# The second product of a spectral mixer and feed-forward kernel: its 21 matmuls per round in threes instead of two passes

## The chip, the cores and the metric

The kernel runs on one core of a Trainium2 chip. A time is the device time of one execution in microseconds (us). Three timed executions took 2598.35, 2600.91 and 2601.14 us; their median, 2600.91 us, is the time before. A fourth execution was recorded by the hardware profiler, and every line of a profile below comes from that one.

## The reference

Two stages follow each other. The first takes x (8 sequences of 3008 tokens, 256 channels), goes to the frequency domain along the tokens, applies one complex 256x256 matrix with a bias and a soft threshold, and goes back. The second is a feed-forward layer on the 24064 tokens:

```python
X = np.fft.rfft(x, axis=1)
Yr = Xr @ w_r - Xi @ w_i + b_r
Yi = Xr @ w_i + Xi @ w_r + b_i
Yr = np.sign(Yr) * np.maximum(np.abs(Yr) - lam, 0.0)   # Yi likewise
y = np.fft.irfft(Y, n=x.shape[1], axis=1)
h = np.maximum(y @ w_in, 0.0)        # 256 -> 2048
out = h * h @ w_out                  # 2048 -> 256
```

## The kernel before

**Operands in two parts.** A float32 operand is split into a high part, rounded to the fast matmul format (fp32r), and a low part, the rest. A product is then three matmuls into the same place of PSUM: high x high, high x low, low x high. The helper `mm3` (L179 to L184) issues them in that order: L182 the high stationary with the high moving operand, L183 the high stationary with the low moving one, L184 the low stationary with the high moving one. The first product of the feed-forward layer, the forward transform (`psa`), the mix (`psm1`, `psm2`) and the way back (`psc`) all go through it, so all their matmuls have the lines L182 to L184 in a profile.

**Rounds.** The tokens are cut into 47 chunks of 512. The hidden 2048 features are cut into 8 pairs of 128-feature blocks. One round is one pair of blocks for one chunk: 47 x 8 = 376 rounds, and one Python loop writes the instructions of every engine in the order in which they are to stand. There is no scheduler behind it; each engine works off its own list in order, and semaphores hold an instruction back until its operands are there and its buffer is free. A round r holds:

- the first product `mm1` into `ph`, two PSUM banks: 12 matmuls of 128x512;
- on ScalarE, `squares`: two relus out of `ph` (L877) and a square (L878) into the tile `g`;
- the second product `mm2` of round r - 3 into `po`, 21 matmuls of 128x256;
- on VectorE, `sums` (L883 to L885), which make the seven operands of a Strassen-like scheme out of `g`;
- on ScalarE `high` (L932), which casts `g` of round r - 1 into `gh`, and on VectorE `low` (L937), which takes the rest into `gl`.

The second product needs 7 sub-products instead of 8 for a 2x2 block product. `PLACES` lists them with their place in the four PSUM banks `po0` to `po3`: two in each of the first three, one in the last. `wo_[0]` and `wo_[1]` are the high and low parts of the combined weights, tiles of 128x7x128 per pair of blocks, in the profile `wo`. `gh` and `gl` have two buffers each, so the cast of round r - 1 goes into the buffer that the product of round r - 3 reads:

```python
def opnd(name, dt, bufs):
    return tl(name, (P, NPR, HALF), dt, bufs=bufs)
```

At a chunk's last round `put_together` copies and adds the seven places into the output tiles (one copy on ScalarE, L903, then seven sums on VectorE, L904 to L910) and sends them out. Bank by bank the last reader is L905 for the first, L906 for the second, L909 for the third and L910 for the fourth; the next chunk's first `mm2` writes the same banks.

**Work around the products.** The transform stage of the next sequences is spread over the rounds by a table and a small planner: places named `p1` (after the first product) and `p2` (after the second) take the matmuls of `psa`, `psb`, `psc`, `psd` and of the mix, and places `e`, `e2`, `f`, `f2`, `a`, `v` take the ScalarE and VectorE steps that belong to them. These matmuls share two PSUM buffers. A pair of frequency rows goes through `psb` in round r0, the mix (18 matmuls of 128x256) in round r0 + 2 and `psc` some rounds later. The mix's first bank is freed by the VectorE sum L233, which stands behind `gl` (L937) in its round. ScalarE's steps of such a round stand behind `gh` (L932): the copy of `psc` (L758), the cast to `xh` (L712), the turns into `z` (L740, L741), the cast to `zh` (L745) and the cast to `fh` (L668).

Of the kernel before, what the change touches and what calls it, by code (L numbers as in the profile page):

```python
# [130 lines left out]
PLACES = ((0, 0, 0), (2, 0, 1), (6, 1, 0), (5, 1, 1), (4, 2, 0), (3, 2, 1), (1, 3, 0))  # L131
NPR = 7
NU = NF // 2
# [3 lines left out]
HALF = CH // 2  # L137
# [12 lines left out]
def fft_mix_moe(ctx: ExitStack, tc: tile.TileContext, xp, xu, w_r, w_i, b_r, b_i,  # L150
                w_in, w_out, t_u, t_a, t_b, t_b0, t_m, t_d, sgn, outT):
    nc = tc.nc
# [19 lines left out]
    wo_ = [], []  # L172
# [6 lines left out]
    def mm3(out, lt, rt, start, stop, **kw):  # L179

        (l0, l1), (r0, r1) = lt, rt
        nc.tensor.matmul(out, l0, r0, start=start, stop=False, **kw)  # L182
        nc.tensor.matmul(out, l0, r1, start=False, stop=False, **kw)  # L183
        nc.tensor.matmul(out, l1, r0, start=False, stop=stop, **kw)  # L184
# [702 lines left out]
    def mm2(j, po, gh, gl):  # L887

        for s, bank, half in PLACES:
            out = po[bank][:, half * HALF:half * HALF + HALF]  # L890
            for k in range(2):
                nc.tensor.matmul(out, wo_[k][j][:, s], gh[:, s], start=j == 0 and half == 0 and k == 0,  # L892
                                 stop=False, skip_group_check=True)
        for s, bank, half in PLACES:
            out = po[bank][:, half * HALF:half * HALF + HALF]
            nc.tensor.matmul(out, wo_[0][j][:, s], gl[:, s], start=False, stop=j == NU - 1,  # L896
                             skip_group_check=True)

    def put_together(c, po):
        p = {s: po[bank][:, half * HALF:half * HALF + HALF] for s, bank, half in PLACES}  # L900
# [15 lines left out]
    with tc.manual_schedule():  # L916
        for r in range(last + LAG):
            c, j = divmod(r, NU)
# [6 lines left out]
            k = r - LAG  # L925
# [15 lines left out]
            if k >= 0:  # L941
                if jj == 0:
                    pos[cc] = [ps_o.tile([P, 512], F32, tag=f"o{i}", name=f"po{i}") for i in range(4)]
                mm2(jj, pos[cc], *split_.pop(k))
# [54 lines left out]
```

## Time and profile before

| | |
|---|---|
| median of three executions | 2600.91 us (2598.35 to 2601.14) |
| the profiled execution | 2604.28 us, span 2602.5 us |
| granted TensorE clock over the span | 0.992 |
| TensorE matmuls, busy | 2540.2 us, 98% |
| VectorE, ScalarE, GpSimd busy | 81%, 77%, 2% |
| DMA queue q1 | 161.91 MB, 20.1% of 16 engines |

The span runs from the first to the last instruction. In a group of instructions the columns are: line, engine, operation, the tile written and the tiles read, shapes, count, then busy time and mean ns of one, then the idle time of the engine just before them and who ended most of it. A row of the timeline has the start in us, the duration in us, the engine, the line, the operation with its tiles, and in brackets the idle time of the engine before it with its releaser; "x14" merges instructions that follow each other. Matmuls overlap, so what one costs is read from the distance of two starts, not from its duration. PEld is the loading of the stationary operand, which runs beside the matmul before it. A row of the waits has the total in us, the number of times and the longest.

### The profile page before, as it was taken

Reading aid. Unit: us, or ns where it says so; the run is one execution under the profiler, and the core shown is the slowest. Engines: PE = TensorE matmul, PEld = TensorE weight load, DVE = VectorE, ACT = ScalarE, POOL = GpSimd, SP = SyncE. Lnnn points to the kernel's source line nnn. Section 1 sums busy time; section 2 is a strip of 40 time slices with the busy share of each in tenths; the row PEclk is TensorE's granted clock in tenths of the full one; section 3 lists DMA queues with packets and bytes.
Section 4 is the critical chain, followed back from the end, with each engine's and each line's share of the span. In section 5 each row is a group of like instructions: output and inputs, shape, how many; then the busy total and the mean of one; then the engine's idle time right before and its main releaser. Section 6 shows DMA issues by size and latency. Waiting matters only on the chain.

```text
span 2602.5 us, 41936 instructions
## 1 busy us (share of the span) xinstructions
PE 2540.2 (98%) x16496; PEld 2284.6 (88%) x16496; DVE 2107.2 (81%) x3155; ACT 1993.8 (77%) x2764; POOL 47.9 (2%) x57
## 2 busy tenths in 40 slices
PE   6979999999999999999999999999999999999999
PEld 3569999999899998999889998899989898999998
DVE  4868888888888888888888888788887888777776
ACT  3668887788778787778877887778777777777776
POOL 1410000000000000000000000000000000000000
PEclk8999999999999999999999999999999999999999
DMA  8621122222221112111122112121121111100000
GB/s 252 186 84 57 49 73 65 78 60 64 76 67 53 55 56 76 57 54 52 57 78 63 55 54 68 56 67 60 44 72 53 41 37 57 37 27 28 20 24 17
DMA packets 113094, 164.59 MB, mean 63 GB/s; under 512 B 9584, under 2 KB 63074, under 8 KB 112706
## 3 DMA queue, kind: packets, MB, share of 16 engines
q1 hardware_dynamic: 112898, 161.91, 20.1%
q8 instruction: 131, 2.15, 0.3%
q14 instruction: 65, 0.53, 0.1%
HBM read 86.90 MB, written 74.97 MB: 62 GB/s over the span
## 4 chain that ended last, share of the span: by engine, by line
PE 82%; DVE 6%; ACT 5%; issue 1%; DMA 1%; DVEq 0%; SPq 0%; ACTq 0%
PE po L892 21%; PE ph L182 12%; PE ph L184 12%; PE ph L183 12%; PE po L896 11%; PE psd L268 3%; PE psb L219 3%; PE psm L182 2%; PE psm L183 2%; PE psm L184 2%; DVE gl L937 2%; ACT g L877 1%; DMA din<-s 1%; ACT g L878 1%; DVE g L883 1%
## 5 line engine op out<-in xcount | busy, mean ns | idle before, releaser
L937 DVE TENSOR_TENSOR gl<-g,gh 128x1792 fp32r<-128x1792 f32 x376 | 760.3, 2022 | 33.8 <-ACT gh L932 24.8
L877 ACT ACTIVATE g<-ph 128x512 f32<-128x512 f32 x752 | 409.2, 596 | 456.0 <-PE ph L184 454.5
L892 PE MATMUL po<-gh,wo 128*128 128x256 f32 x5264 | 700.9, 283 | 1.4 <-DVE o L909 0.8
L892 PEld LDWEIGHTS po<-gh,wo 128*128 128x128 f32 x5264 | 656.6, 188 | 15.1 <-DVE o L909 4.3
L932 ACT CAST gh<-g 128x1792 fp32r<-128x1792 f32 x376 | 638.4, 1698 | 19.9 <-PE po L892 16.6
L182 PE MATMUL ph<-xt,wi 128*128 128x512 f32 x1504 | 592.3, 394 | 11.2 <-DVE dx L276 8.7
L184 PE MATMUL ph<-xt,wi 128*128 128x512 f32 x1504 | 588.2, 391 | 0.0
L183 PE MATMUL ph<-xt,wi 128*128 128x512 f32 x1504 | 587.5, 391 | 0.0
L883 DVE TENSOR_TENSOR g<-g 128x512 f32<-128x512 f32 x376 | 260.0, 691 | 328.2 <-ACT g L878 325.9
L878 ACT ACTIVATE g<-g 128x1024 f32<-128x1024 f32 x376 | 399.5, 1062 | 11.9
L896 PE MATMUL po<-gl,wo 128*128 128x256 f32 x2632 | 371.3, 280 | 0.0
L184 PEld LDWEIGHTS ph<-xt,wi 128*128 128x128 f32 x1504 | 282.7, 188 | 64.4
L182 PEld LDWEIGHTS ph<-xt,wi 128*128 128x128 f32 x1504 | 282.9, 188 | 62.2 <-ACT xt L280 8.8
L896 PEld LDWEIGHTS po<-gl,wo 128*128 128x128 f32 x2632 | 336.8, 188 | 0.0
L183 PEld LDWEIGHTS ph<-xt,wi 128*128 128x128 f32 x1504 | 282.9, 188 | 50.5
L885 DVE TENSOR_TENSOR g<-g 128x256 f32<-128x256 f32 x376 | 160.0, 425 | 12.9
L884 DVE TENSOR_TENSOR g<-g 128x256 f32<-128x256 f32 x376 | 159.9, 425 | 12.8
L182 PE MATMUL psm<-wm,xh 128*128 128x256 f32 (+1 forms) x552 | 161.4, 292 | 3.7 <-DVE dx L276 3.2
L183 PE MATMUL psm<-wm,xh 128*128 128x256 f32 (+1 forms) x552 | 159.2, 288 | 0.0
L184 PE MATMUL psm<-wm,xl 128*128 128x256 f32 (+1 forms) x552 | 159.0, 288 | 0.0
L219 PEld LDWEIGHTS psb<-tB,bin 128*128 128x128 f32 x768 | 100.6, 194 | 36.0 <-issue 17.8
L268 PEld LDWEIGHTS psd<-tD,din 120*128 120x128 f32 (+1 forms) x832 | 107.4, 191 | 19.1 <-DMA din<-s 8.9
(102 smaller groups left out, 2569.7 us busy)
## 6 DMA issues: line engine op xcount, KB each, us to landing
bin<-s SPq DMA_DIRECT2D x96, 256.0 KB
s<-evc SPq DMA_DIRECT2D x96, 256.0 KB
outT_dram<-o SPq DMA_DIRECT2D x94, 256.0 KB
din<-s SPq DMA_DIRECT2D x96, 240.0 KB
xin<-in_xp_dram SPq DMA_DIRECT2D x72, 240.0 KB
s<-eva SPq DMA_DIRECT2D x72, 240.0 KB
s<-eva SPq DMA_DIRECT2D x22, 192.0 KB
w<-in_moe_w_in_dram SPq DMA_DIRECT2D x8, 512.0 KB
```

What stands on the lines that cost most here:

```text
L182: nc.tensor.matmul(out, l0, r0, start=start, stop=False, **kw)
L183: nc.tensor.matmul(out, l0, r1, start=False, stop=False, **kw)
L184: nc.tensor.matmul(out, l1, r0, start=False, stop=stop, **kw)
L219: nc.tensor.matmul(ps[:, k, :, q, :], tv[:, q, k], tB[:, 0:r + 2:r + 1], start=True, stop=True)
L268: nc.tensor.matmul(ps[:, k, part], t[:n, s:s + P], tD[:n, tab + part, :n], start=True, stop=True)
L877: nc.scalar.activation(g[:, 2 * a:2 * a + 2], ph[:, a].rearrange("p (t m) -> p t m", t=2), AF.Relu)
L878: nc.scalar.activation(g[:, 0:4], g[:, 0:4], AF.Square)
L883: nc.vector.tensor_sub(g[:, 4:6], g[:, 1:4:2], g[:, 0:2])
L892: nc.tensor.matmul(out, wo_[k][j][:, s], gh[:, s], start=j == 0 and half == 0 and k == 0, stop=False, skip_group_check=True)
L896: nc.tensor.matmul(out, wo_[0][j][:, s], gl[:, s], start=False, stop=j == NU - 1, skip_group_check=True)
L932: nc.scalar.copy(split_[r - 1][0], hid[r - 1])
L937: nc.vector.tensor_sub(gl, hid.pop(r - 1), gh.bitcast(F32))
```

## The change

`mm2` issued its 21 matmuls in two passes: first, place by place, the high and the low weights with the high operand `gh` (14 matmuls, L892), then the high weights with the low operand `gl` (7 matmuls, L896). Now it issues three per place through `mm3`. The matmuls are the same; their order is not. The place on which the first matmul of a chunk clears its bank and the one that ends it are set by the same conditions as before.

```diff
     def mm2(j, po, gh, gl):
 
         for s, bank, half in PLACES:
-            out = po[bank][:, half * HALF:half * HALF + HALF]
-            for k in range(2):
-                nc.tensor.matmul(out, wo_[k][j][:, s], gh[:, s], start=j == 0 and half == 0 and k == 0,
-                                 stop=False, skip_group_check=True)
-        for s, bank, half in PLACES:
-            out = po[bank][:, half * HALF:half * HALF + HALF]
-            nc.tensor.matmul(out, wo_[0][j][:, s], gl[:, s], start=False, stop=j == NU - 1,
-                             skip_group_check=True)
+            mm3(po[bank][:, half * HALF:half * HALF + HALF], (wo_[0][j][:, s], wo_[1][j][:, s]),
+                (gh[:, s], gl[:, s]), j == 0 and half == 0, j == NU - 1, skip_group_check=True)
```

The lines behind it move up by six: L932 and L937 of before are L926 and L931 afterwards.

TensorE at the end of a second product, here the last one of the kernel; `wo07` is the high and `wo17` the low part of the weights of pair 7. Before:

```order
L892 MATMUL po3_26309<-gh_26515,wo07_1097 128x256
L892 MATMUL po3_26309<-gh_26515,wo17_1098 128x256
L896 MATMUL po0_26306<-gl_26516,wo07_1097 128x256 x2
L896 MATMUL po1_26307<-gl_26516,wo07_1097 128x256 x2
L896 MATMUL po2_26308<-gl_26516,wo07_1097 128x256 x2
L896 MATMUL po3_26309<-gl_26516,wo07_1097 128x256
```

With the change:

```order
L184 MATMUL po2_26308<-gh_26515,wo17_1098 128x256
L182 MATMUL po2_26308<-gh_26515,wo07_1097 128x256
L183 MATMUL po2_26308<-gl_26516,wo07_1097 128x256
L184 MATMUL po2_26308<-gh_26515,wo17_1098 128x256
L182 MATMUL po3_26309<-gh_26515,wo07_1097 128x256
L183 MATMUL po3_26309<-gl_26516,wo07_1097 128x256
L184 MATMUL po3_26309<-gh_26515,wo17_1098 128x256
```

The last reader of `gh` was the 14th matmul of the 21 and is now the 21st; the last of `gl` was the 21st and is now the 20th. The first reader of `gl` was the 15th and is now the 2nd.

TensorE in the first product of the last chunk, where the banks come free one after the other. Before, from the 7th matmul on:

```order
L892 MATMUL po1_26307<-gh_26201,wo00_719 128x256
L892 MATMUL po1_26307<-gh_26201,wo10_720 128x256
L892 MATMUL po2_26308<-gh_26201,wo00_719 128x256
L892 MATMUL po2_26308<-gh_26201,wo10_720 128x256
L892 MATMUL po2_26308<-gh_26201,wo00_719 128x256
```

With the change, from the 10th on:

```order
L182 MATMUL po1_26307<-gh_26201,wo00_719 128x256
L183 MATMUL po1_26307<-gl_26202,wo00_719 128x256
L184 MATMUL po1_26307<-gh_26201,wo10_720 128x256
L182 MATMUL po2_26308<-gh_26201,wo00_719 128x256
L183 MATMUL po2_26308<-gl_26202,wo00_719 128x256
```

The third bank, `po2`, is written for the first time by the 9th matmul before and by the 13th now, and the first bank is finished by the 16th before and by the 6th now. On ScalarE, VectorE, GpSimd and SyncE the instructions stand in the same order as before; what `gh` waits for on TensorE is another matmul.

## The prediction

> **What bounds the kernel now.** I read the page first: the busy time, then the chain that ended last.
>
> ```profile
> PE 2540.2 (98%) x16496; PEld 2284.6 (88%) x16496; DVE 2107.2 (81%) x3155; ACT 1993.8 (77%) x2764; POOL 47.9 (2%) x57
> PE 82%; DVE 6%; ACT 5%; issue 1%; DMA 1%; DVEq 0%; SPq 0%; ACTq 0%
> L892 PE MATMUL po<-gh,wo 128*128 128x256 f32 x5264 | 700.9, 283 | 1.4 <-DVE o L909 0.8
> L896 PE MATMUL po<-gl,wo 128*128 128x256 f32 x2632 | 371.3, 280 | 0.0
> L932 ACT CAST gh<-g 128x1792 fp32r<-128x1792 f32 x376 | 638.4, 1698 | 19.9 <-PE po L892 16.6
> ```
>
> TensorE carries 82% of the chain. The edited product is 5264 + 2632 = 7896 matmuls, 21 in each of 376 rounds, and none of them ever waited for gl. The third group row is the one to remember: ScalarE's cast into gh is held up by matmuls of L892. There are two gh buffers, so a cast waits until the product two rounds older has read the same buffer for the last time.
>
> Then the waits, for the places where TensorE is not its own bound, and for the slack of the other two:
>
> ```profile
> ACT g L877 <- PE ph L184: 454.5, 267, 4.6
> PEld psb L219 <- DVE e L233: 11.2, 14, 1.3
> PE psb L219 <- DVE e L233: 5.7, 10, 0.9
> PEld po L892 <- DVE o L909: 4.3, 16, 0.5
> PE psd L268 <- DMA din<-s: 7.9, 8, 1.8
> PE psm L182 <- DVE dx L276: 3.2, 4, 0.9
> ```
>
> In 267 rounds ScalarE waits for the first product (1.7 us in the mean), so it can absorb a delay there; in the other 109 it arrives late. TensorE waits for VectorE ten times at psb, because the mix's first bank is freed late by L233.
>
> **The change, part by part.** It removes and adds no instruction, byte or DMA; it permutes 21 matmuls. Four things follow.
>
> *(a) Spacing of the matmuls.* Read from the timeline as starts:
>
> ```profile
> 1318.60 0.28 PE L182 MATMUL psa<-fh,tAs 120*120 120x256 f32 x1
> ...
> 1319.31 1.81 PE L892 MATMUL po<-gh,wo 128*128 128x256 f32 x14
> ...
> 1320.96 0.99 PE L896 MATMUL po<-gl,wo 128*128 128x256 f32 x7
> ```
> ```profile
> 906.35 0.28 PE L182 MATMUL psm<-wm,xh 128*128 128x256 f32 x1
> ...
> 908.40 0.40 PE L182 MATMUL ph<-xt,wi 128*128 128x512 f32 x1
> ```
>
> The 14 matmuls of L892 go in pairs on one output, the seven of L896 each on another: (1320.96 - 1319.31) / 14 = 0.118 us. The forward transform goes in threes already: six matmuls in 1319.31 - 1318.60 = 0.71 us, again 0.118 us each. But the mix, in threes with the same 128x256 form, takes 2.05 / 18 = 0.114 us in this round. So the order in threes is seen at both spacings. I take no change, since psa has the product's kind of operands (constant weights, fresh moving data). The bounds: at the mix's spacing 7896 x 0.0041 = 32 us less; at 0.120 us, the rounded first step of psa, 7896 x 0.002 = 16 us more.
>
> *(b) gh is released later.* Today the 14th matmul is gh's last reader, afterwards the 21st. The round in which that bites:
>
> ```profile
> 911.96 1.90 PE L892 MATMUL po<-gh,wo 128*128 128x256 f32 x14
> ...
> 913.69 0.99 PE L896 MATMUL po<-gl,wo 128*128 128x256 f32 x7
> 913.90 1.70 ACT L932 CAST gh<-g 128x1792 fp32r<-128x1792 f32 x1
> ...
> 919.12 1.08 ACT L877 ACTIVATE g<-ph 128x512 f32<-128x512 f32 x2
> ```
> ```profile
> 921.33 0.70 DVE g L883
> ...
> 930.73 2.02 DVE gl L937
> 932.75 0.61 DVE e L233
> ...
> 933.40 1.16 PE psb L219 x8
> ```
>
> The cast starts at 913.90, 0.04 us after L892's end at 911.96 + 1.90 = 913.86. With the new order it must wait for the end that L896 has today, 913.69 + 0.99 = 914.68: 0.78 us later. Queued behind it on ScalarE are the store's copy, xh, the four turns and fh, with no wait among them, and then the next relu at 919.12, which has no wait ahead of it either (the row names none). So relu, the square, VectorE's sums at 921.33, the putting together of the chunk, two gl casts and L233 all start 0.78 us later, and psb on TensorE with them. The second fence is the chain that ended last over that stretch: it runs from this cast to that psb. All ten waits of psb for L233 have this shape, a chunk's end in the stretch between a pair's first round and its mix, so 10 x 0.78 = 7.8 us.
>
> Most other rounds absorb it. A mix round without a chunk's end:
>
> ```profile
> 1204.83 0.98 PE L896 MATMUL po<-gl,wo 128*128 128x256 f32 x7
> ...
> 1205.46 1.69 ACT L932 CAST gh<-g 128x1792 fp32r<-128x1792 f32 x1
> ...
> 1209.12 0.68 DVE L233 TENSOR_TENSOR e<-psm,bias 128x512 f32<-128x512 f32 x1
> ...
> 1210.45 1.05 PE L219 MATMUL psb<-tB,bin 128*128 128x128 f32 x8
> ```
>
> Here the cast moves by 1205.81 - 1205.46 = 0.35 us, and L233 ends 1210.45 - 1209.80 = 0.65 us before psb needs it. The four short psb waits that only the weight load shows (14 against 10) and the four psm waits for L276 have part of the delay left; I take 8 x 0.15 = 1.2 us, between 0 (all absorbed) and 8 x 0.78 = 6.2 us. The transfers of din are behind ScalarE's store copies, so their eight waits could grow by up to 6.2 us too; I take 0, since that row names the transfer alone, and keep the 6.2 us for the range.
>
> gl is needed earlier, as the 2nd matmul instead of the 15th, 13 x 0.118 = 1.5 us. In the steady state it costs nothing: the gl that starts at 930.73 is read two rounds later, and a round takes 2602.5 / 376 = 6.9 us. Its buffer's release moves from the 21st matmul to the 20th; nobody waits for that.
>
> *(c) Banks of the output.* A chunk's first product waits for the last one's sums. The third bank is written first by the 9th matmul today, afterwards by the 13th, 4 x 0.118 = 0.47 us later, which covers waits of this size:
>
> ```profile
> 2565.27 2.13 PE L892 MATMUL po<-gh,wo 128*128 128x256 f32 x14
> ...
> 2566.42 0.77 PEld L892 LDWEIGHTS po<-gh,wo 128*128 128x128 f32 x6 [0.25 <-DVE o L909]
> ```
>
> 14 matmuls took 2.13 instead of 1.81 us. Of the 16 such waits ten lie in the stretches of (b), where VectorE sets the end and TensorE would only wait longer at psb; the six chunk ends after 2300 us give 6 x 0.32 = 1.9 us back.
>
> *(d) The end.* The last three products have no first product between them:
>
> ```profile
> 2590.54 4.11 DVE L937 TENSOR_TENSOR gl<-g,gh 128x1792 fp32r<-128x1792 f32 x2
> 2590.64 0.99 PE L896 MATMUL po<-gl,wo 128*128 128x256 f32 x7
> 2590.88 1.71 ACT L932 CAST gh<-g 128x1792 fp32r<-128x1792 f32 x1 [0.40 <-PE po L892]
> ...
> 2593.94 1.81 PE L892 MATMUL po<-gh,wo 128*128 128x256 f32 x14
> ...
> 2596.02 0.37 ACT L903 COPY o<-po 128x256 f32<-128x256 f32 x1 [3.43 <-PE po L896]
> ```
>
> The last gh cast moves to 2591.65, the last gl to 2593.37, ending at 2595.4; the second matmul of the last product waits for it, and the last matmul starts 19 x 0.118 later, at 2597.7 instead of 2596.3: 1.4 us. Against that, the first bank is now finished by the 6th matmul, not the 16th, so L903 starts at about 2596.3 and its seven sums run while the other banks finish; L904, which needs the 12th matmul, starts near 2597.0 instead of 2596.43. Net +0.5 us.
>
> **Sum:** 0 + 7.8 + 1.2 - 1.9 + 0.5 = +7.6 us. The profiled execution took 2604.28 us for a span of 2602.5, which would become 2611.9; it lies 3.4 us above the median of the three timed runs, 2600.91, so I expect 2609 us.
>
> **Rivals.**
>
> *The order changes the spacing for the better* (15%): the mix's 0.114 us holds for the product too. For it: same form, same order. Against it: psa in threes at 0.118, and a mix in threes at (763.98 - 761.86) / 18 = 0.118 as well, so the order alone does not decide:
>
> ```profile
> 761.86 0.28 PE L182 MATMUL psm<-wm,xh 128*128 128x256 f32 x1
> ...
> 763.98 0.40 PE L182 MATMUL ph<-xt,wi 128*128 128x512 f32 x1
> ```
>
> 2609 - 32 = 2577 us, faster than before. It decides from a gain of 2 ns per matmul, where it outweighs (b).
>
> *The delay is absorbed* (22%): idle slots on ScalarE and VectorE that the rows round away, and the bank relief also in the ten stretches. Then (b) gives 1 us, and 2601 us stays.
>
> *The spacing gets worse* (7%): 0.120 us throughout, 2609 + 16 = 2625 us.
>
> *The clock halves* (9%). One wait today did this:
>
> ```profile
> 1674.23 1.12 PE L268 MATMUL psd<-tD,din 120*128 120x120 f32 x8 [1.76 <-DMA din<-s]
> ...
> 1675.11 2.79 PE L892 MATMUL po<-gh,wo 128*128 128x256 f32 x14
> ...
> 1674.00:1678.00 4.00, 3.77 (x24) 3.81 (x25) 3.16 (x8) 1.50 (x4) 0.00 (x0) 0.72 0.25 69
> ```
>
> After 1.76 us without a matmul the granted clock fell to 0.72 in the next 4 us, and that round's 14 matmuls took 2.79 instead of 1.81 us; with the seven behind them about 1.6 us were lost. The long psb waits of 0.9 us would grow to 1.3 and 1.7 us. If five of them cross the line, 5 x 1.6 = 8 us more: 2617 us. The Trainium skill (TensorE: Matmul & The Clock Gate, "Why this matters for your kernels") says that gaps of TensorE up to about 3 us leave the clock alone; by it this rival has no chance and the sum stays. The row above shows a drop after a gap shorter than that, so the trace does not agree, and I keep the rival.
>
> **How the numbers follow.** The forecast has 47%, its own range 2603 to 2615: (b) at 0.35 us an event, without the remainder, to (b) with its upper ends. Faster or slower by 0.2% (5.2 us) is about what a measurement of this kernel can tell from no change. Slower takes 44 of the forecast's 47, 2 of the absorbed case and the two dear rivals: 62%. Faster takes the good spacing and 2 of the absorbed case: 17%. The rest, 21%, is no change. The range of 2596 to 2619 leaves out the good spacing and the dearest cases.
>
> **What would show it.** Right: the gh cast waits for the 21st matmul in far more than 26 rounds, by up to 0.8 us; psb's waits for L233 grow from 5.7 to about 13 us, still around ten; L909's waits vanish after 2262 us; 21 matmuls still take 2.48 us. Wrong: a product round whose 21 matmuls take 2.39 us or less, or psb's waits unchanged although the cast starts later.

## The result and the profile after

The changed kernel takes 2622.97 us, the median of three executions (2621.94 to 2623.69), against 2600.91: a ratio of 1.0087, 95% interval 1.0065 to 1.0110. It is slower, as forecast, by 22 us instead of 8, and outside the range. Its profiled execution took 2623.69 us with a span of 2621.8, so between the two profiles there are 19.3 us of span to explain. Before's profiled execution lay 3.4 us above its median, after's lies 0.7 above; that is the other 2.7 us. Two of the series below, the change once more and both repairs in the changed kernel, hold one execution each at a lower clock (2792.83 and 4165.58 us): their medians are over all executions, which moves them by under 0.3 us, and their ratios leave it out.

The page of the changed kernel: busy time, then a group with busy time, mean ns of one and idle time ahead.

```profile
PE 2546.2 (97%) x16496; PEld 2283.8 (87%) x16496; DVE 2109.9 (80%) x3155; ACT 2007.0 (77%) x2764; POOL 47.9 (2%) x57
L183 PE MATMUL po<-gl,wo 128*128 128x256 f32 x2632 | 735.4, 279 | 1.3 <-DVE gl L931 1.3
```

Its waits (total in us, times, longest):

```profile
ACT g L877 <- PE ph L184: 344.6, 223, 4.2
ACT gh L926 <- PE po L184: 151.2, 246, 2.1
PE psb L219 <- DVE e L233: 11.7, 14, 1.4
PE ph L182 <- ACT g L877: 6.7, 12, 1.2
PE psd L268 <- DMA din<-s: 5.6, 8, 1.7
PE po L182 <- ACT xt L280: 2.1, 5, 0.5
PE po L182 <- DVE o L899: 1.9, 5, 0.9
```

The cast into `gh` waited for the product 26 times and 16.6 us before; now 246 times and 151.2 us. That idle time mostly comes out of the time in which ScalarE had waited for the first product (454.5 us before, 344.6 now), which costs nothing by itself. What reaches TensorE is small and sits in few rows: the waits at psb doubled as forecast, from 5.7 to 11.7 us, and a row that was forecast nowhere appeared: the first product itself waits for ScalarE's relu, 12 times and 6.7 us (2 times, 2.4 us before).

The forecast's own place, the stretch whose cast started at 913.90 before, in the timeline of the changed kernel:

```profile
916.30 0.36 PE L182 MATMUL po<-gh,wo 128*128 128x256 f32 x1
...
919.05 1.69 ACT L926 CAST gh<-g 128x1792 fp32r<-128x1792 f32 x1 [0.71 <-PE po L184]
```

and the end of that stretch in the chain of waits that ended last:

```profile
937.88 0.61 DVE e L233
938.53 1.16 PE psb L219 x8
```

From the product's first matmul to the cast it was 913.90 - 911.96 = 1.94 us; it is 919.05 - 916.30 = 2.75, so 0.81 later. From the cast to psb it was 933.40 - 913.90 = 19.50 us and is 938.53 - 919.05 = 19.48: the whole stretch moved as one piece.

The new place, a round without a chunk's end. Before, and then after:

```profile
836.70 0.62 ACT L668 CAST fh<-f 120x512 fp32r<-120x512 f32 x1
837.22 1.08 ACT L877 ACTIVATE g<-ph 128x512 f32<-128x512 f32 x2
...
838.53 0.40 PE L182 MATMUL ph<-xt,wi 128*128 128x512 f32 x1
```
```profile
835.78 1.69 ACT L926 CAST gh<-g 128x1792 fp32r<-128x1792 f32 x1 [0.71 <-PE po L184]
...
839.03 0.28 PE L182 MATMUL po<-gh,wo 128*128 128x256 f32 x1
...
840.46 0.62 ACT L668 CAST fh<-f 120x512 fp32r<-120x512 f32 x1
840.99 1.08 ACT L877 ACTIVATE g<-ph 128x512 f32<-128x512 f32 x2
...
841.39 0.28 PE L184 MATMUL po<-gh,wo 128*128 128x256 f32 x1
842.12 0.50 PE L182 MATMUL ph<-xt,wi 128*128 128x512 f32 x1 [0.46 <-ACT g L877]
```

Before, the second of the two relus ended at 837.22 + 1.08 = 838.30 and the next first product began at 838.53, with no wait shown: some 0.2 us of slack. Now the cast waits 0.71 us, all of ScalarE's list behind it is late, and the relus end at 842.07; the first product begins 0.05 us after that, having waited. `ph` is one tile of two banks, and its first matmul waits until both relus have read it. Comparing the starts of the first product round by round, nine rounds of this kind lose 0.63 us each.

Where the span's 19.3 us went, from that comparison of starts (376 differences, grouped by place):

| place | us |
|---|---|
| ten stretches with a chunk's end, 0.71 to 0.95 each: 5.0 where psb waits for L233, 2.9 at the first matmul of the new chunk | +7.9 |
| nine rounds in which the first product waits for the relu, 0.63 each | +5.7 |
| the four short psb waits (0.34 to 0.45) and four rounds from 495 to 620 us (0.25 to 0.49) | +3.2 |
| other single rounds (largest 0.63, 0.59, 0.38) | +2.7 |
| steps below 0.12 us over all other rounds, 2.1 of it within the first product | +3.5 |
| six chunk ends after 2300 us, 0.32 each | -1.9 |
| the round of the low clock near 1676 us, which was only in before's profile; 0.5 of it is a longer wait for the transfer | -2.1 |
| start and end | +0.4 |

### The profile page after: what moved, and what is told of

Its sections match the earlier page's. It is cut to its first block, busy times and chain, and to the rows that moved or that the text cites. A ratio compares the mean times of both kernels' runs of the same rounds, so it can differ in the third digit from the quotient of the medians.

```text
span 2621.8 us, 41621 instructions
## 1 busy us (share of the span) xinstructions
PE 2546.2 (97%) x16496; PEld 2283.8 (87%) x16496; DVE 2109.9 (80%) x3155; ACT 2007.0 (77%) x2764; POOL 47.9 (2%) x57
## 4 chain that ended last, share of the span: by engine, by line
PE 78%; DVE 8%; ACT 7%; DMA 3%; issue 3%; SPq 0%; DVEq 0%; ACTq 0%
PE ph L182 11%; PE ph L184 10%; PE ph L183 10%; PE po L184 10%; PE po L182 10%; PE po L183 10%; PE psb L219 3%; PE psd L268 3%; PE psm L182 2%; DVE gl L931 2%; PE psm L183 2%; PE psm L184 2%; ACT g L877 2%; ACT z L741 1%; DMA din<-s 1%
## 5 line engine op out<-in xcount | busy, mean ns | idle before, releaser
L931 DVE TENSOR_TENSOR gl<-g,gh 128x1792 fp32r<-128x1792 f32 x376 | 760.6, 2023 | 139.5 <-ACT gh L926 137.0
L926 ACT CAST gh<-g 128x1792 fp32r<-128x1792 f32 x376 | 638.3, 1698 | 161.0 <-PE po L184 151.2
L182 PE MATMUL po<-gh,wo 128*128 128x256 f32 x2632 | 751.7, 286 | 4.0 <-ACT xt L280 2.1
L183 PE MATMUL po<-gl,wo 128*128 128x256 f32 x2632 | 735.4, 279 | 1.3 <-DVE gl L931 1.3
L184 PE MATMUL po<-gh,wo 128*128 128x256 f32 x2632 | 735.5, 279 | 0.0
L877 ACT ACTIVATE g<-ph 128x512 f32<-128x512 f32 x752 | 408.5, 595 | 346.1 <-PE ph L184 344.6
L182 PEld LDWEIGHTS po<-gh,wo 128*128 128x128 f32 x2632 | 494.4, 188 | 12.2 <-ACT xt L280 3.5
L183 PEld LDWEIGHTS po<-gl,wo 128*128 128x128 f32 x2632 | 494.5, 188 | 6.3 <-DVE gl L931 1.5
L184 PEld LDWEIGHTS po<-gh,wo 128*128 128x128 f32 x2632 | 494.0, 188 | 0.0
```

What stands on the lines that cost most here:

```text
L877: nc.scalar.activation(g[:, 2 * a:2 * a + 2], ph[:, a].rearrange("p (t m) -> p t m", t=2), AF.Relu)
L926: nc.scalar.copy(split_[r - 1][0], hid[r - 1])
L931: nc.vector.tensor_sub(gl, hid.pop(r - 1), gh.bitcast(F32))
```

## The experiments

Two causes could stand behind the table: the release of `gh` (with two ways to TensorE, the mix's first bank and the tile `ph`), and the order as such (spacing, banks, an early `gl`). The runs were timed beside the kernel before on the same chip, where it took 2601.95, 2602.66 or 2601.83 us.

**The change once more**, beside the other versions:

> The changed kernel once more, on the chip of the next three. Theory (release): 2623 us, 1.0085 of before, since the cast into gh waits for the 21st matmul. Rival (order): the same. It is the reference for the runs beside it.

It took 2623.66 us, a ratio of 1.0081 (1.0067 to 1.0094).

**Only the late release.** The two passes of before stay; one matmul, the low weights with `gh` of the last place, moves from the 14th position to the 21st. `gl` is read as late as before, and no threes are formed:

```diff
-            for k in range(2):
+            for k in range(1 if s == late else 2):
...
+        nc.tensor.matmul(out, wo_[1][j][:, late], gh[:, late], start=False, stop=j == NU - 1,
+                         skip_group_check=True)
```

> The two passes of before, with one matmul moved: the last place's low weights with gh go from the 14th to the 21st position. gl is still first read by the 14th matmul, and the third bank is still written first by the 9th. Theory (gh's release decides): the loss of the change without its gains at the banks (1.9 us) and with all its waits, so 2623 to 2627 us. Rival (the order in threes, or gl read by the 2nd matmul, costs the time): one matmul moved costs nothing, 2601 us.

2624.11 us, 1.0085 (1.0071 to 1.0099). Moving one matmul in 21 costs all that the change costs. Its waits:

```profile
ACT gh L935 <- PE po L899: 160.4, 250, 2.1
PE psb L219 <- DVE e L233: 6.9, 14, 0.9
PE ph L182 <- ACT g L877: 6.9, 11, 1.7
PE po L893 <- DVE o L912: 2.5, 10, 0.3
```

The cast and the relu are held as in the changed kernel, and the nine rounds lose 0.62 to 0.64 us each in the comparison of starts. The third bank is written as early as before, so the wait for it stands (last row). The ten stretches lose 7.9 us again, but nearly all of it here, in the chunk's first product, and only 0.2 at psb. After 2300 us the starts move by nothing where the changed kernel gets 1.9 us back.

**The size of the delay.** The first places in threes, the others in two passes, so that the last reader of `gh` is the 18th matmul (four places) or the 15th (one place). `gl` is read as the 2nd matmul in both:

```diff
+        for p in PLACES[:4]:
+            one(p, 0, gh, False)
+            one(p, 0, gl, False)
+            one(p, 1, gh, True)
+        for p in PLACES[4:]:
+            one(p, 0, gh, False)
+            one(p, 1, gh, False)
+        for p in PLACES[4:]:
+            one(p, 0, gl, True)
```

> Threes for the first four places, then the pairs with gh of the other three, then their gl. gh is last read by the 18th matmul, so its cast moves by 4 x 0.118 = 0.47 us instead of 0.83; gl is read by the 2nd matmul as in the change, and the third bank is written first by the 13th. Theory (release, beyond a slack of 0.2 us for the first product): ten psb waits x 0.47 + nine first products x 0.27 + about 2, less 2 at the banks: 2608 to 2612 us. Rival (gl early or threes): four of seven places in threes and gl as early, so 2614 to 2623 us. Rival (all or nothing): 2623 us.

> Only the first place in threes, the rest in two passes as before. gl is read by the 2nd matmul, as in the change, but gh is last read by the 15th, one later than before. Theory (release): ten psb waits x 0.12 = 1.2 us more, nothing at the first product, 0.7 us less at the banks, 1.0 us more at the end: 2602 to 2605 us. Rival (gl early): about what the change lost, 2615 us or more.

Four places: 2609.40 us, 1.0030 (1.0019 to 1.0041). One place: 2602.53 us, 1.0001 (0.9993 to 1.0010). The waits of the first, and of the second:

```profile
ACT gh L938 <- PE po L891: 76.0, 154, 1.8
PE psb L219 <- DVE e L233: 10.6, 10, 1.4
```
```profile
ACT gh L938 <- PE po L891: 27.1, 58, 1.4
```

| last reader of `gh` | 14th | 15th | 18th | 21st |
|---|---|---|---|---|
| 0.118 us x positions later | 0 | 0.12 | 0.47 | 0.83 |
| cost, us (beside before on the same chip) | 0 | -0.1 | 7.5 | 21.7 |

The costs include what the banks give back, 0.7 us with one place and 1.9 with four or seven. The cost grows faster than the delay, since each place has its own slack. With four places the nine rounds lose 0.27 to 0.29 us each, which is 0.63 less 3 x 0.118; with one place they lose nothing. So their slack was about 0.2 us (0.83 - 0.63). The ten stretches have less than 0.1 us each: they lose 0.4 us in all with one place, 4.2 with four and 7.9 with seven. The small remainder has more. The early `gl` costs nothing outside the end of the kernel: one place in threes already has it, and there it costs 1.1 us, 0.9 of it a wait of the last product for `gl`.

**The way over `ph`.** The changed kernel, with `ph` as two tiles of one bank, in the same two PSUM banks:

```diff
-        ph = ps_h.tile([P, 2, CH], F32, tag="h", name="ph")
+        ph = [ps_h.tile([P, CH], F32, tag=f"h{a}", name="ph") for a in range(2)]
```

> The changed kernel with the first product's two banks as two tiles, so that its first matmul waits for the first relu alone and no longer for both. Theory: nine waits of 0.63 us of the first product for the relu in the changed kernel came from the second relu; they go, and the small ones like them: 2615 to 2618 us, with psb's waits for L233 as they are, about 14 us by starts. Rival (the first product would wait for the first relu as well): 2623 us.

2616.18 us, 1.0056 (1.0043 to 1.0070): 7.5 us less than the change beside it. The waits:

```profile
PE psb L219 <- DVE e L233: 11.8, 14, 1.4
ACT gh L926 <- PE po L184: 244.7, 264, 2.1
```

The relu's wait row of 6.7 us fell to 1.0 us (two times), the nine rounds got 0.48 to 0.49 us back each (4.4 us), and psb's row stayed at 11.8. Of the other 3 us about one is at the start, before 200 us. The total came as expected, but only 4.4 us of it came by the way that the theory names; a later run showed that the split gives about as much where hardly any first product waits for the relu.

**The way over the mix's first bank.** In a mix round the two VectorE sums L233 and L234 go ahead of `gl` instead of behind it, in the changed kernel and in the one before:

```diff
-            else:
+            elif r not in mixes:
                 low()
             run(r, "f")
             run(r, "f2")
-            if ends:
+            if ends or r in mixes:
                 low()
```

> The changed kernel, and in the rounds with a mix VectorE frees the mix's banks (L233, L234) ahead of its cast into gl instead of behind it. gh's release is untouched. Theory: the delay reaches psb only through gl and L233, so the psb waits for L233 (14 us) go and the first product's waits for the relu stay: 2607 to 2612 us. Rival (the delay reaches TensorE by the ScalarE steps alone): 2620 us or more.

> The same move of L233 and L234 in the kernel before. Theory: its psb waits for L233, 9 us by starts, go: 2592 to 2595 us. Rival (VectorE's total sets the end of those stretches, so the wait goes elsewhere): 2600 us.

With the change: 2608.01 us, 1.0024 (1.0015 to 1.0033), 5.4 us above the kernel before instead of 21.7. Without it: 2592.67 us, 0.9962 (0.9950 to 0.9975), 10.0 us below; by the comparison of starts the ten stretches give 0.52 to 1.16 us each, 8.3 in all. VectorE of the latter in the stretch shown before, with the psb that needs L233:

```profile
928.23 0.68 DVE L233 TENSOR_TENSOR e<-psm,bias 128x512 f32<-128x512 f32 x1
...
929.63 2.02 DVE L937 TENSOR_TENSOR gl<-g,gh 128x1792 fp32r<-128x1792 f32 x1
```
```profile
929.86 1.05 PE L219 MATMUL psb<-tB,bin 128*128 128x128 f32 x8
```

L233 ends at 928.91, psb starts 0.95 us later without a wait, and no row of psb waiting for L233 is left. With the change the row falls from 11.7 to 1.0 us, while the relu's row stays:

```profile
PE psb L219 <- DVE e L233: 1.0, 4, 0.3
PE ph L182 <- ACT g L877: 7.0, 11, 1.7
```

The two runs stood on the same chip, 15.3 us apart. So most of what this move gives the changed kernel it gives the other one too; from the loss of 21.7 us it takes 6.4. In the comparison of starts the 5.0 us at psb are gone, and at the first matmuls of the ten chunks 3.3 us remain.

**Both repairs**, in the changed kernel:

> The changed kernel with both repairs: two tiles for the first product's banks, and the mix's banks freed ahead of gl. Theory: the two losses are separate paths behind the same cast, so the gains add: 2616 - 14 = 2602 us, within 3 us, without touching gh's release. Rival (one path hides behind the other): 2606 us or more.

2601.35 us, 0.9993 (0.9984 to 1.0002): no difference from the kernel before that can be measured. The number came as expected, but it doesn't show that the two ways carry the loss, because the repairs may speed up a kernel without the change as well. The next run is the one to set beside it.

**Both repairs in the kernel before**, and the same with two places in threes, which leaves the banks' relief and releases `gh` two matmuls later:

> The kernel before with both repairs: the mix's banks freed ahead of gl, and two tiles for the first product's banks. Theory: with gh released by the 14th matmul the first product is not held up by the relu in the main part, so the second repair adds nothing: 2591 to 2594 us, as with the first repair alone (2592.7). Rival (the relu has slack to give everywhere): 2589 us or less.

> Both repairs, and the second product with its first two places in threes, the rest in two passes: gh is last read by the 16th matmul (0.24 us later than before), and the third bank is written first by the 11th (0.24 us later). Theory: the 16 waits at a chunk's first product, 0.32 us each, shrink to 0.1 us, and the later gh finds slack once the two paths are repaired: 3 us less than before_both, 2588 to 2591 us. Rival (gh's release costs as much as the banks give): 2592 us or more.

The first took 2584.48 us, 0.9936 (0.9923 to 0.9948), and is the best version; the second 2588.26 us, 0.9948 (0.9934 to 0.9961). The first was a miss: the two tiles of `ph` were expected to give nothing where no first product waits for the relu, and gave some 7 us (17.4 below the kernel before, against 10.0 with the mix first alone; 6.8 between the two spans, 2591.5 and 2584.7). The second fell into its expected figures, but the comparison behind them came out the other way: with the better kernel beside it, the threes lose 3.8 us. The timeline of ScalarE shows the miss. One tile (before with the mix first), its first product starting at 1203.52, and two tiles, starting at 1201.78:

```profile
1203.52 0.40 PE L182 MATMUL ph<-xt,wi 128*128 128x512 f32 x1
...
1206.46 1.09 ACT L877 ACTIVATE g<-ph 128x512 f32<-128x512 f32 x2 [3.50 <-PE ph L184]
```
```profile
1201.78 0.40 PE L182 MATMUL ph<-xt,wi 128*128 128x512 f32 x1
...
1203.36 0.60 ACT L877 ACTIVATE g<-ph 128x512 f32<-128x512 f32 x1 [2.56 <-PE ph L184]
...
1204.72 0.60 ACT L877 ACTIVATE g<-ph 128x512 f32<-128x512 f32 x1 [0.76 <-PE ph L184]
```

The tile binds both ways. With one tile the first relu waits for all 12 matmuls and starts 2.94 us after the first of them; with two it waits for six and starts after 1.58 us. The pair ends 3.54 us after the product's start instead of 4.03, and all of ScalarE's and VectorE's list is that much earlier: the six waits for L909 after 2300 us go (0.32 us each in the comparison of starts), and the waits for the transfer shrink, from 8.4 us (8 times) to the last row here. In this version, and with two places in threes:

```profile
ACT gh L932 <- PE po L892: 61.4, 147, 1.3
PE psd L268 <- DMA din<-s: 5.8, 4, 2.0
```
```profile
ACT gh L938 <- PE po L891: 111.0, 230, 1.5
```

With the relu earlier, the cast waits for the product in 147 rounds instead of the 16 with one tile, so the release of `gh` now limits ScalarE more often; with two threes it does so 230 times. That the threes lose there for this reason is the reading that fits; no run took it alone. The 3 us that the split gave in the changed kernel beside the nine rounds may be of the same kind; how they divide among places was not settled.

**What the change costs beside a kernel with the same repairs.** Each time is given as its distance, in us, from the kernel before on the same chip:

| | without the change | with the change | the change costs |
|---|---|---|---|
| no repair | 0 | +21.7 | 21.7 |
| mix first | -10.0 | +5.4 | 15.3 |
| both repairs | -17.4 | -1.3 | 16.0 |

The repairs pay with and without the change, and with both in place the change still costs 16.0 us, 15.0 between the two spans. So they make up for the loss and do not remove its cause: the cast waits for the product in 270 rounds with the change and in 147 without. TensorE's waits with both repairs and the change, and then without the change:

```profile
PE psd L268 <- DMA din<-s: 7.5, 7, 2.0
PE psm L182 <- DVE dx L276: 3.1, 3, 1.2
PE po L182 <- ACT xt L280: 2.2, 5, 0.6
PE po L182 <- DVE o L899: 1.9, 5, 1.0
PE psb L219 <- DVE e L233: 1.1, 4, 0.3
```
```profile
PE psm L182 <- DVE dx L276: 1.9, 4, 0.6
PE po L892 <- DVE o L909: 0.7, 3, 0.3
```

In the comparison of starts, the 15.0 us are 3.3 at the first matmuls of ten chunks, 2.5 at five psb waits, 4.7 ahead of the mix's first matmul, 2.5 at the transfers of din, 1.3 in the nine rounds and 0.7 elsewhere. The late release thus reaches TensorE by more ways than the two that were repaired. How far the part of the transfers belongs to it is open: moving the mix first in the kernel before shifted it by 1.5 us too.

By this account a third buffer for `gh` should take away the wait that all these ways start from. No run tried it.

## The prediction, point by point

**(a) Spacing: right.** The 21 matmuls from 839.03 to 841.39 take 0.118 us each, 2.48 us in all, as before; after 2300 us the median from the first start to the last is 2.36 us in both kernels. Both rivals built on another spacing fall with that.

**(b) Release of gh: the mechanism right, one of its ways missed, the remainder too small.** The cast waits for the 21st matmul in 246 rounds. The ten stretches were to cost 7.8 us and cost 7.9; 2.9 of it shows already at the chunk's first product, so psb's row grew to 11.7 us and not to 13. The step that failed is "Most other rounds absorb it". It looked from the delayed relu along VectorE to L233, and judged the relu's slack by the 267 rounds in which ScalarE waits for the first product. That is a total, and says nothing of the rounds that lack the slack; the other 109 it named and gave no price. In the nine rounds, where the forward transform's cast `fh` stands ahead of the relu, ScalarE's list from the cast to the relu has no gap, and 0.2 us behind the relu's end the next first product writes the same tile: 838.30 and 838.53 stood in the trace of before. Nine rounds x 0.63 = 5.7 us stand against nothing. The remainder is the other term that was too small: 8 x 0.15 = 1.2 us with an upper end of 6.2, against some 9 us outside the stretches and the nine rounds. Of that, 1.5 us is at the four short psb waits, 1.7 in the early rounds, where in three of the four the mix now waits for ScalarE's copy L223, and 2.7 in other single rounds, the two largest at a wait for L276 and at one for the transfer. The last 3.5 us are small steps, of which the runs show no cause. The transfers of din did not grow in all: 7.9 to 5.6 us.

**(c) Banks: right.** Six times 0.32 us came back, the waits for L909 in the middle of a product are gone after 2300 us, and the ten ends within the stretches gave nothing. There the chunk's first matmul waits instead, in five rounds for L899, the last reader of the first bank (1.9 us), and in five for the cast L280, which ends 0.06 us behind L899 (2.1 us); this lies inside the ten stretches' 7.9 us.

**(d) The end: right within its size.** The last product's second matmul waits for `gl`, 1.3 us, and the sums follow as worked out:

```profile
2612.02 2.03 DVE L931 TENSOR_TENSOR gl<-g,gh 128x1792 fp32r<-128x1792 f32 x1 [0.48 <-ACT gh L926]
2615.72 0.42 DVE L898 TENSOR_TENSOR o<-po,o 128x256 f32<-128x256 f32 x1 [1.67 <-PE po L184]
```

The first sum starts 1.67 us after `gl` ends; the forecast had 1.6. The end costs some 0.7 us, not 0.5.

**The rivals.** *Absorbed* is refuted: the loss is there, and dosing the delay doses it. *The clock halves* did not happen: psb's longest wait grew from 0.9 to 1.4 us, and the granted clock there stayed at 1.00 (the last window below). The one drop in before's profile did not come again; if the timed runs lacked it too, its round accounts for 2.1 of the 2.7 us by which the two profiles differ less than the medians.

## What to carry over

When the last reader of a double-buffered operand moves later, follow the writer's engine down its list to every point at which the bottleneck waits for it, and judge each by the slack of that round; a total of idle time over hundreds of rounds hides the rounds that have none. A tile with two writers or two readers is one lock in both directions: splitting it by bank let the reader start after half of the work and freed the bank earlier, which gave some 7 us even where the first product hardly ever waited for the bank. And a repair shows a cause only beside the same repair in the unchanged kernel: here both repairs brought the changed kernel level with the one before, and the change still cost 16 us beside a kernel with both.

## What was not expected of the hardware

The clock fell after one wait and not after others nearly as long. In the trace of before it was 0.72 for the 4 us behind a wait of 1.76 us, as shown in the prediction. The record of the clock in that trace is sharper: half clock from 1675.78 to 1679.19, which is 3.41 us. Its five other spells at half clock ahead of 151 us last 3.41, 10.24 or 17.07 us, each a whole number of 3.41. Cut at these steps, the windows (length, busy time and count of TensorE, its loads, VectorE, ScalarE, GpSimd; granted clock, DMA share, GB/s) show the step that holds the wait and the one behind it:

```profile
1672.40:1675.80 3.40, 1.64 (x15) 1.60 (x15) 1.53 (x5) 2.90 (x5) 0.00 (x0) 1.00 0.45 139
1675.80:1679.20 3.40, 3.40 (x19) 3.40 (x18) 2.26 (x6) 1.26 (x1) 0.00 (x0) 0.50 0.61 176
```

The kernel before with the mix first has a wait of 1.67 us at the same kind of transfer. It too lies wholly within one step, if the steps are counted on from that trace's last change of clock at 148.4 us, and the clock stays:

```profile
1349.87 1.12 PE L268 MATMUL psd<-tD,din 120*128 120x120 f32 x8 [1.67 <-DMA din<-s]
```
```profile
1346.50:1349.90 3.40, 1.73 (x9) 1.12 (x7) 2.03 (x3) 1.63 (x3) 0.00 (x0) 1.00 0.66 181
1349.90:1353.30 3.40, 3.40 (x30) 3.40 (x31) 2.70 (x7) 1.94 (x4) 0.00 (x0) 1.00 0.22 51
```

In the changed kernel one of the longest waits at psb leaves it alone as well:

```profile
1260.00:1264.00 4.00, 2.65 (x19) 2.15 (x17) 3.83 (x5) 2.54 (x4) 0.00 (x0) 1.00 0.23 84
```

In the step of the drop TensorE was busy for 1.64 of 3.40 us, in the other for 1.73. So the two cases lie on either side of half a step, but one drop is no threshold. The Trainium skill (TensorE: Matmul & The Clock Gate, "Why this matters for your kernels") warns only of gaps of TensorE above about 3 us: the waits up to 1.67 us agree with it, the one of 1.76 us does not.
